# A new stored order for an attention and spatial-gate kernel on one core

## The chip, the cores and the metric

The kernel runs on one core of one Trainium2 chip. Its time is what the device takes for one execution, in microseconds (us); the median of three runs stands for the kernel before.

## The reference

```python
# q, k, v: (8 batches, 8 heads, 576 positions, 64)
# coarse attention: q, k, v averaged over groups of 4 positions
out_d = softmax(scale * q_d @ k_d.T) @ v_d          # 144 positions
out_up = repeat(out_d, 4)
# local attention: only positions with |i - j| < 4
out_local = softmax(where(mask, scale * q @ k.T, -1e9)) @ v
x = (out_up + out_local) as (8, 576, 512)
# gated unit over 576 positions
h = gelu(x @ w_in)                                  # (8, 576, 1024), tanh form
u, v = h[..., :512], h[..., 512:]
v_n = layer_norm(v) * g_ln
v_s = einsum('ts,bsd->btd', w_sg, v_n) + b_sg       # mixes positions
out = x + (u * v_s) @ w_out
```

## The kernel before

**Stages.** The attention goes by pairs of heads, 32 in all, numbered 4 times the batch plus the pair. For one pair the kernel loads four arrays (q, k, two forms of v), sums q and k over groups of four positions (lines 596 to 600), multiplies scores for both attentions into banks of PSUM (lines 625 to 653), adds the mask (640), takes maxima (662 to 676), exponentials (692 to 714), sums and reciprocals (719 to 725), normalises (728, 736), transposes by matmuls (739, 748), copies out of PSUM (248), multiplies with v (800, 816) and adds the two results (781 to 787, 823). The gated unit goes by batches: 931 (924 in the first batch) multiplies into v, 1132 and 1143 into u, 1086 mixes the positions with w_sg, 1267 multiplies with w_out, 1274 adds x. Every float32 product is made of products of a rounded high part and a low part, so many pieces are splits of an array: a cast (248) and a subtraction (835, 1021, 1250, 424, 535).

**Pieces and their names.** A program is 2,448 pieces; a name is a kind, a number and sometimes a chunk. Those that the prediction speaks of: `D1` is the product with v of pair 1, and the products of `D9` those of pair 9 (lines 800 and 816); `YS10` the coarse and local scores of pair 10 (653 and 632); `ma9` and `mb9` the mask addition (640), `qs10` the sums of q (596), `my9` maxima (674, 676), `od7` a scaling (787), `mx9` maxima (664), `xa7` and `xb7` the addition of two results (823). `v1.2` is a chunk of the second batch's product into v (931), `u1.2` of its product into u (1132), `s1.01` the first product of its mixing of positions (1086). `sa0.4` and `sa0.7` take the first batch's mixed values out of PSUM (1185), and `sa7.4` and `sa7.6` the last batch's (1120), `sm0.4` applies such a value to the gate (1194). `wlr1` and `wbr3` are steps in splitting w_out (424; 407 and 409), `sg` guards the small gain vector of 128 by 4 (339 to 341), `gt` guards the gain row of 64 by 512 and takes its reciprocal (339 to 341, 349), `ta1` to `ta4` combine parts of w_sg (516), `tl` and its like split them (535, 556), `oa0.0` adds x into an output of the first batch (1226). `gd7` and `gl7.1` make a factor of the last batch's output products (1238, 1250), `o7.12` and `s7.14` are products of that batch (1267, 1086).

**What sets the order.** The string `ORDER` holds all pieces in one sequence. `place` (lines 69 to 87) walks through it: each word names a piece and, behind a slash, the engine where there is a choice (V is VectorE, A ScalarE, P GpSimd). A piece that needs a buffer takes the one that has been free for longest, out of 8 banks of PSUM ("ps"), 10 buffers "X" or 38 buffers "R", and the last reader in the sequence gives it back. The loop at lines 1452 to 1460 emits the pieces in that sequence with the automatic scheduler off, so each engine runs its pieces in the order of the string, and a piece waits for its inputs and for the last reader of the buffer that it got. Ahead of `S0` and `S3` the loop puts 28 and 20 matmuls of zeros (line 1459). All loads and stores go out on the queue of SyncE (SP), and each waits for the sixth before it (`DEPTH = 6`).

Of the kernel before, what the change touches and what calls it, by code (L numbers as in the profile page):

```python
# [90 lines left out]
lq0 lk0 ks0 qs0 S0 mx0 ia0 ib0 lk1 ea0 Y0 my0 ny0 lq1 S1 qs1/P lk2 mx1 es0 ia1 lq2 S2 ks1/P ib1 ks2/P qs2/P lq3 lk3 ec0  # L91
re0 rc0 Y1 qs3/P my1 mx2 S3 ea1 es1 nq0 ks3/P wy0 wqy0 wby0 ia2 ib2 ny1 np0 wuy0 ec1 wy2 wqy2 U0 re1 wuy2 lk4 wy1 rc1
wty0 np1 ea2 T0 pa0 pb0 mx3 ia3 ib3 Y2 ks4/P my2 wqy1 pc0 ea3 lv0 es2 T1 t0 ny2 lq4 es3 ec2 pe0 Y3 re2 my3 ny3 pa1 rc2
nq1 t1 lw0 U1 ec3 qs4/P wuy1 pb1/V pc1 wby2 D0 wby1 oe0 od0 re3 rc3 YS4 xa0 pe1 ma4 mb4 wz0 wuz0 xb0 lv1 why0 nq2 np2 U2
wqz0 T2 pa2 wty2 lk5 why2 t2 pb2 np3 T3 wty1 pa3 pc2 lw1 D1 pe2/V nq3 mx4 nx4 eb4 wly2 wz3 wqz3 lv2 ks5 wbz0 oe1/V lq5
lw3 my4 ny4 U3 pb3 ec4 vk0.0 t3 vk3.0 lv3 od1 xa1 xb1 pc3 pe3 qs5 wbz3 wuz3 why1/V ea4 vk0.1 YS5 my5 vk1.0 vk1.1 ny5
wtz0 ec5 wy3 wqy3 lw2 vs2 vk2.0 vk2.1 wtz3 D2 ma5 mb5 mx5 re4/V rc4 wby3 nx5 oe2/V od2 vs3 D3 np4 vk3.1 wuy3 wty3 xa2
xb2 wly0 oe3/V wz1 od3 xa3 vk1.2 xb3 eb5 ea5 lv4 whz3/V wlz3 wuz1 lw4 re5 vk2.2 v0.2 v0.1 whz0/V wlz0 rc5 nq5 vs4/V np5
wqz1 nq4/A vg0.2 t4 why3 U4 wly3 T4 pa4 pb4/V vb0.2/A pc4/V pe4 lk6 ks6 lq6 wz2 vk3.2 wbz1 v0.3 wtz1 lk7 vp0.2 wq2 vg0.1
wqz2 vg0.3 vk0.2 v0.0 vg0.0 ks7/P qs6 vb0.0/A wuz2 wbz2 wtz2 vb0.1/A T5 vp0.1 pa5/V D4 YS6 lq8 U5 oe4/V od4 vk4.0 vk4.1  # L100
# [1422 lines left out]
```

## Time and profile before

| | us |
|---|---|
| runs | 555.56, 552.9, 556.1; median 555.56 |
| profiled execution | 553.21, of which the span is 551.4 |
| TensorE, matmuls | 538.7 busy, 98% of the span |
| VectorE | 475.1 busy, 86% |
| ScalarE | 428.7 busy, 78% |
| GpSimd | 366.4 busy, 66% |

The granted clock of TensorE is 1.00 in all stretches. PE is TensorE, PEld its load of weights, DVE VectorE, ACT ScalarE, POOL GpSimd, SP SyncE. The span of 551.4 us is cut below into five stretches by hand: up to 41 us the first loads, the splits of w_in and the first four pairs; to 95 us the first batch's gated unit; to 152 us the end of that and the splits of w_out and w_sg; to 537 us the batches that follow, all alike; and the last output products. An idle time is put down to whatever the engine's next instruction waited for last.

### The profile page before, as it was taken

What the parts mean: (1) busy time and instruction counts of PE and PEld (TensorE: products, weight loads), DVE (VectorE), ACT (ScalarE), POOL (GpSimd) and SP (SyncE); (2) the same over time, 40 slices, a digit from 0 to 9 for tenths busy, and PEclk for the clock granted to TensorE, in tenths of its full rate; (3) what the DMA queues carried; (4) which work ended last, traced back from release to release, by engine and by line L of the source; (5) the groups of instructions that cost most, each with busy time, mean ns of one, the idle gap of its engine ahead of it and who ended that gap; (6) DMA issues with size and microseconds to landing.
All of it is one profiled execution on the core that took longest, in us unless ns stands there. A gap on an engine that the chain in (4) does not pass through costs nothing.

```text
span 551.4 us, 17280 instructions
## 1 busy us (share of the span) xinstructions
PE 538.7 (98%) x6720; PEld 490.6 (89%) x6720; DVE 475.1 (86%) x970; ACT 428.7 (78%) x1457; POOL 366.4 (66%) x435
## 2 busy tenths in 40 slices
...
GB/s 313 265 308 291 81 195 207 167 68 59 129 153 100 21 172 60 178 23 90 142 129 122 76 171 99 57 50 61 140 147 149 1 102 116 65 1 1 23 65 87
DMA packets 31923, 64.62 MB, mean 117 GB/s; under 512 B 3744, under 2 KB 4768, under 8 KB 31840
## 3 DMA queue, kind: packets, MB, share of 16 engines
...
q14 instruction: 30, 0.25, 0.1%
...
## 4 chain that ended last, share of the span: by engine, by line
PE 82%; DVE 10%; issue 3%; POOL 2%; ACT 1%; DMA 1%; SPq 1%; DVEq 0%; POOLq 0%
PE ps L1086 16%; PE ps L931 16%; PE ps L1267 14%; PE ps L1132 14%; PE ps L924 3%; PE ps L800 3%; PE ps L1143 3%; PE ps L816 3%; PE ps L739 3%; PE ps L632 3%; PE ps L748 2%; PE ps L653 2%; PE ps L1459 1%; DMA X<-in_vw_dram 1%; DVE R L1021 1%
## 5 line engine op out<-in xcount | busy, mean ns | idle before, releaser
L1132 PE MATMUL ps<-X,weight_z 128*128 128x288 f32 x448 | 95.6, 297 | 0.0
L692 ACT ACTIVATE X<-X,nb 128x64 f32<-128x64 f32 x280 | 93.5, 338 | 0.6 <-DVE nb L671 0.2
L931 PE MATMUL ps<-weight_y,X 128*128 128x512 f32 x280 | 84.8, 396 | 0.3 <-DVE R L409 0.3
L1132 PEld LDWEIGHTS ps<-X,weight_z 128*128 128x128 f32 x448 | 73.7, 188 | 0.4 <-DVE R L1226 0.2
L1132 PE MATMUL ps<-R,weight_z 128*128 128x288 f32 x224 | 66.1, 295 | 0.0
L931 PEld LDWEIGHTS ps<-weight_y,X 128*128 128x128 f32 x280 | 51.0, 188 | 10.7 <-PE ps L632 0.4
L1086 PE MATMUL ps<-wsg_h,R 128*128 128x288 f32 x266 | 58.5, 300 | 1.5 <-DVE X L640 0.7
L248 ACT CAST R<-R 128x512 fp32r<-128x512 f32 (+2 forms) x81 | 50.3, 642 | 11.9 <-PE ps L1132 2.3
L1274 DVE TENSOR_TENSOR R<-ps,R 128x288 f32<-128x288 f32 x98 | 42.3, 449 | 19.2 <-PE ps L1267 18.8
L692 ACT ACTIVATION_READ_ACCUMULATOR X<-X,nb 128x1 f32 x280 | 53.2, 190 | 0.0
L1021 POOL TENSOR_TENSOR R<-R,R 128x512 fp32r<-128x512 f32 (+1 forms) x24 | 32.0, 1338 | 28.9 <-ACT R L248 15.2
L1267 PE MATMUL ps<-R,weight_r 128*128 128x288 f32 x336 | 50.7, 296 | 0.0
L1267 PEld LDWEIGHTS ps<-R,weight_r 128*128 128x128 f32 x336 | 47.1, 188 | 1.4
L248 ACT COPY R<-ps 128x464 f32<-128x464 f32 (+4 forms) x94 | 33.5, 395 | 17.4 <-PE ps L739 13.5
L1086 PEld LDWEIGHTS ps<-wsg_h,R 128*128 128x128 f32 x266 | 43.7, 188 | 2.8 <-issue 0.9
L931 PE MATMUL ps<-weight_y,R 128*128 128x512 f32 x112 | 44.3, 396 | 0.0
L728 POOL TENSOR_TENSOR X<-X,rc 128x640 f32<-128x640 f32 x25 | 33.1, 1325 | 14.7 <-DVE rc L725 11.6
L1132 PEld LDWEIGHTS ps<-R,weight_z 128*128 128x128 f32 x224 | 42.2, 188 | 0.0
L1166 ACT ACTIVATE R<-ps 128x288 f32<-128x288 f32 x64 | 24.1, 414 | 23.1 <-PE ps L1132 21.4
L1250 POOL TENSOR_TENSOR R<-R,R 128x576 fp32r<-128x576 f32 x19 | 29.0, 1535 | 15.3 <-ACT R L248 9.6
L1267 PE MATMUL ps<-R,R 128*128 128x288 f32 x252 | 37.5, 298 | 0.0
L613 DVE TENSOR_REDUCE vd<-R 112x128 f32<-112x512 f32 x36 | 37.3, 1076 | 0.0
...
## 6 DMA issues: line engine op xcount, KB each, us to landing
...
```

The costliest lines, as they stand in the source:

```text
L248: (nc.scalar.copy if e == "A" else ENG[e].tensor_copy)(**kw)
L613: nc.vector.tensor_reduce(out=vd[:, i], in_=v.rearrange("p f d -> p d f"), axis=AX.X, op=ALU.add)
L692: nc.scalar.activation(out=st["ms"][:, t, :], in_=src, func=AF.Exp, bias=st["nb"][:, t:t + 1], scale=scale, accum_out=sums[par][:, t:t + 1])
L728: ENG[e].tensor_tensor(out=st["ms"], in0=st["ms"], in1=bc_last(st["rc"][:, 0:NT], KB), op=ALU.mult)
L931: nc.tensor.matmul(out=acc, lhsT=r32(l), rhs=r32(weights[f"y{k}"][:, 0, w]), start=(i == 0 and ks[0] == 0), stop=(i == len(ops) - 1 and ks ...
L1021: ENG[e].tensor_tensor(out=r32(dst), in0=vact[s][0][0:n], in1=vh[0:n, 0:DM], op=ALU.subtract)
L1086: nc.tensor.matmul(out=s_bank(j, c), lhsT=r32(l), rhs=r32(r), start=first_in and i == 0, stop=i == len(ops) - 1, skip_group_check=not firs ...
L1132: nc.tensor.matmul(out=acc[:, 0:HALF], lhsT=r32(l), rhs=r32(r), start=(first and n == 0), stop=(last and n == len(ops) - 1))
L1166: nc.scalar.activation(out=gate(i), in_=at["ps", "m", b, "u", i][:, 0:HALF], func=AF.Gelu_apprx_tanh)
L1250: ENG[e].tensor_tensor(out=r32(gl[m]), in0=us[raws[m]], in1=gh[m], op=ALU.subtract)
L1267: nc.tensor.matmul(out=bank(j, c), lhsT=r32(l), rhs=r32(r), start=first and i == 0, stop=i == len(ops) - 1, skip_group_check=not first)
L1274: nc.vector.tensor_tensor(out=x, in0=bank(j, c), in1=x, op=ALU.add)
```

## The change

The string `ORDER` is replaced in whole, lines 91 to 213; no other line differs. The pieces are the same 2,448. Their sequence differs: 558 of them stand more than 20 places from where they stood, 201 at most. 346 of them run on another engine: 101 go from VectorE to ScalarE, 85 from ScalarE to VectorE, 76 from GpSimd to VectorE, 60 from VectorE to GpSimd, 13 from GpSimd to ScalarE and 11 from ScalarE to GpSimd. Since buffers are handed out along the string, other pieces share a buffer. One line of the table before and one now, both from its end:

```diff
--- before.py
+++ after.py
@@ -88,123 +88,123 @@
 
 
 ORDER = """
...
-o7.15 ua7.6 sa7.6 gl7.0 o7.11 sa7.4 gh7.1/A gd7/V gh7.4/A gl7.1/V oa7.15 o7.05 o7.02 gl7.4/V o7.01 os6.2 os6.1 gh7.6/A
...
+ua7.6 gl7.3/V s7.04 s7.14 sa7.6 sa7.4 gh7.1/A gd7/V os6.1 o7.01 gl7.1/V oa7.00 gl7.4/V o7.15 o7.05 oa7.15 gh7.6/A o7.12
...
```

Three places in the order follow. A row is a line of the program, an operation, what it writes and reads (with the number of the buffer and of its use) and the tile's shape.

**VectorE near the end of the first batch's mixing of positions**, before. Lines 674 and 676 are `my9`, 823 `xa7` and `xb7`, 596 `qs10`, 424 `wlr1`, 339 to 341 `sg`, 1185 `sa0.7`, which frees the bank that `YS10` gets, and 407 and 409 `wbr3`, which frees the bank of `v1.2`:

```order
L674 TENSOR_REDUCE stats1_94<-ps2_1702 128x2
L676 TENSOR_REDUCE stats1_94<-ps4_1703 128x1
L823 TENSOR_TENSOR R34_1809<-ps1_1672,od21_92 128x5x58
L823 TENSOR_TENSOR R34_1809<-ps5_1673,od21_92 128x5x58
L596 TENSOR_REDUCE qd0_89<-R11_1806 128x144
L424 TENSOR_TENSOR weight_r1_1773<-R24_1244,weight_r1_1773 128x2x256
L339 TENSOR_SCALAR g_tmp_78<-g_sb_74 128x4
L340 SCALAR_TENSOR_TENSOR g_tmp_78<-g_sb_74,g_tmp_78 128x4
L341 TENSOR_TENSOR g_sb_74<-g_sb_74,g_tmp_78 128x4
L1185 SCALAR_TENSOR_TENSOR wst3l_121<-ps6_1836,g_sb_74,wst3h_75 128x288
L407 TENSOR_SCALAR ps7_1855<-weight_r3_1635 128x512
L409 SCALAR_TENSOR_TENSOR R13_1856<-weight_r3_1635,ps7_1855 128x512
```

and now (the first row is `sa0.4`, the second `mx9`):

```order
L1185 SCALAR_TENSOR_TENSOR wst3l_121<-ps4_1751,g_sb_74,wst3h_75 128x288
L664 TENSOR_REDUCE stats1_94<-X7_1744 128x10
L823 TENSOR_TENSOR R4_1816<-ps6_1673,od21_92 128x5x58
L823 TENSOR_TENSOR R4_1816<-ps7_1674,od21_92 128x5x58
L339 TENSOR_SCALAR g_tmp_78<-g_sb_74 128x4
L340 SCALAR_TENSOR_TENSOR g_tmp_78<-g_sb_74,g_tmp_78 128x4
L341 TENSOR_TENSOR g_sb_74<-g_sb_74,g_tmp_78 128x4
L1194 TENSOR_TENSOR R8_1254<-R8_1254,wst3l_121 128x288
L424 TENSOR_TENSOR weight_r1_1668<-R1_1280,weight_r1_1668 128x2x256
L1185 SCALAR_TENSOR_TENSOR wst3l_121<-ps2_1800,g_sb_74,wst3h_75 128x288
L407 TENSOR_SCALAR ps6_1858<-weight_r3_1615 128x512
L409 SCALAR_TENSOR_TENSOR R16_1859<-weight_r3_1615,ps6_1858 128x512
```

The guard `sg` moved ahead of `wlr1`, and `sm0.4` (line 1194) came to VectorE between them; `qs10` (596), `my9` (674, 676) and `od7` (787), which stood behind `sa0.4`, now stand ahead of it, above the first row shown.

**VectorE between the reciprocal of the gain row and the first batch's output**, before. 516 are `ta1` to `ta4`, 1226 are the additions of x to the first batch's output:

```order
L516 TENSOR_TENSOR R30_2245<-R18_1951 128x288
L516 TENSOR_TENSOR R30_2245<-R26_2243 128x288
L1226 TENSOR_TENSOR R19_618<-ps4_2193,R19_618 128x288
L556 TENSOR_TENSOR wsdl_86<-R27_2085,wsdh_85 64x288
L516 TENSOR_TENSOR R13_2274<-R31_2272,R18_1951 128x288
L516 TENSOR_TENSOR R13_2274<-R5_1949,R26_2243 128x288
L516 TENSOR_TENSOR R11_2277<-R31_2272,R30_2245 128x288
L516 TENSOR_TENSOR R11_2277<-R5_1949,R30_2245 128x288
L516 TENSOR_TENSOR R28_2284<-R31_2272,R11_2277 128x288
L516 TENSOR_TENSOR R28_2284<-R5_1949,R11_2277 128x288
L725 RECIPROCAL rc0_108<-sums0_95 128x13
L535 TENSOR_TENSOR wsg_l_80<-R30_2245,wsg_h_79 128x2x288
```

and now:

```order
L516 TENSOR_TENSOR R26_2234<-R35_2232 128x288
L516 TENSOR_TENSOR R26_2234<-R10_2059 128x288
L516 TENSOR_TENSOR R15_2237<-R28_2000,R26_2234 128x288
L516 TENSOR_TENSOR R15_2237<-R32_2207,R26_2234 128x288
L1226 TENSOR_TENSOR R23_725<-ps7_2194,R23_725 128x288
L516 TENSOR_TENSOR R33_2250<-R28_2000,R35_2232 128x288
L516 TENSOR_TENSOR R33_2250<-R32_2207,R10_2059 128x288
L516 TENSOR_TENSOR R16_2257<-R28_2000,R15_2237 128x288
L516 TENSOR_TENSOR R16_2257<-R32_2207,R15_2237 128x288
L556 TENSOR_TENSOR wsdl_86<-R30_2020,wsdh_85 64x288
L248 CAST wst4h_83<-R16_2257 128x576
L1226 TENSOR_TENSOR R22_713<-ps4_2271,R22_713 128x288
```

The last addition of the first batch, `oa0.0`, reads the bank that `u1.2` gets next; it now stands behind all of `ta1` to `ta4`, line 556 and a cast, and line 535 went elsewhere.

**The queue of loads (SP) for w_sg, the gain row and the bias rows**, before:

```order
L240 DMA R12_1946<-in_b_rows_dram 64x576
L240 DMA R5_1949<-in_w_sgT_dram 128x576
L240 DMA R18_1951<-in_w_sgT_dram 128x576
L240 DMA R20_2002<-in_kT_dram 128x586
L240 DMA R16_2012<-in_qT_dram 128x586
L240 DMA R29_2050<-in_qT_dram 128x586
L240 DMA R27_2085<-in_w_sgT_dram 128x576
L240 DMA R11_2087<-in_v4_dram 112x512
L240 DMA R28_2088<-in_v4_dram 112x512
L240 DMA R33_2135<-in_g_row_dram 64x512
L240 DMA R26_2243<-in_w_sgT_dram 128x576
L240 DMA R31_2272<-in_w_sgT_dram 128x576
```

and now:

```order
L240 DMA R28_2000<-in_w_sgT_dram 128x576
L240 DMA R30_2020<-in_w_sgT_dram 128x576
L240 DMA R32_2039<-in_kT_dram 128x586
L240 DMA R10_2059<-in_w_sgT_dram 128x576
L240 DMA R9_2098<-in_qT_dram 128x586
L240 DMA R37_2135<-in_qT_dram 128x586
L240 DMA R26_2137<-in_v4_dram 112x512
L240 DMA R15_2138<-in_v4_dram 112x512
L240 DMA R17_2166<-in_g_row_dram 64x512
L240 DMA R32_2207<-in_w_sgT_dram 128x576
L240 DMA R35_2232<-in_w_sgT_dram 128x576
L240 DMA R35_2300<-in_b_rows_dram 64x576
```

The bias rows were the first of this stretch and are now the last, in the buffer that a part of w_sg had; the gain row keeps its place behind two loads of v, in a buffer that `D9` reads last.

## Rows read from the trace of the kernel before

**Rows 1.** The page's part 1, all engines: busy us, share of the span, instructions
```profile
PE 538.7 (98%) x6720; PEld 490.6 (89%) x6720; DVE 475.1 (86%) x970; ACT 428.7 (78%) x1457; POOL 366.4 (66%) x435
```

**Rows 2.** Windows, us: busy time (instructions) of each engine, granted clock, DMA share, GB/s
```profile
0.00:41.00 41.00, 35.96 (x722) 26.34 (x723) 33.77 (x95) 30.04 (x114) 32.46 (x50) 1.00 0.92 294
41.00:95.00 54.00, 53.25 (x711) 40.99 (x709) 48.83 (x104) 49.99 (x164) 46.34 (x48) 1.00 0.61 193
95.00:152.00 57.00, 54.16 (x650) 49.85 (x649) 55.42 (x106) 47.33 (x162) 35.43 (x41) 1.00 0.36 110
152.00:537.00 385.00, 384.20 (x4562) 362.51 (x4561) 328.60 (x650) 298.34 (x1016) 247.94 (x295) 1.00 0.29 90
537.00:551.40 14.40, 11.18 (x84) 10.91 (x82) 8.47 (x18) 2.97 (x5) 4.28 (x4) 1.00 0.24 84
```

**Rows 3.** Waits of TensorE, whole span: us in total, times, longest us
```profile
PE ps L653 <- DVE wst3l L1185: 1.6, 1, 1.6
PE ps L739 <- issue: 1.3, 1, 1.3
PE ps L739 <- POOL X L728: 1.2, 2, 0.9
...
PE ps L800 <- issue: 0.8, 1, 0.8
PE ps L1086 <- DVE X L640: 0.7, 1, 0.7
...
PE ps L748 <- POOL pd L736: 0.4, 1, 0.4
```

**Rows 4.** Timeline of TensorE: start, length, work, [idle before <- releaser]
```profile
102.66 0.52 PE L653 MATMUL ps<-kd,qd 64*64 64x144 f32 x12 [1.59 <-DVE wst3l L1185]
...
104.09 0.70 PE L931 MATMUL ps<-weight_y,X 128*128 128x512 f32 x2 [0.26 <-DVE R L409]
...
114.66 0.22 PE L816 MATMUL ps<-R,X 64*64 64x58 f32 x1
...
130.59 1.58 PE L1132 MATMUL ps<-R,weight_r 128*128 128x288 f32 x10 [0.25 <-DVE R L1226]
...
151.44 0.50 PE L1086 MATMUL ps<-wsg_h,R 128*128 128x288 f32 x2 [0.74 <-DVE X L640]
```

**Rows 5.** Timeline of VectorE, around the first wait, columns as above
```profile
95.03 0.52 DVE L1185 SCALAR_TENSOR_TENSOR wst3l<-ps,g_sb,wst3h 128x288 f32<-128x288 f32 x1 [0.62 <-PE ps L1132]
...
99.13 1.39 DVE L339 TENSOR_SCALAR g_tmp<-g_sb 128x4 f32<-128x4 f32 x1
...
102.09 0.52 DVE L1185 SCALAR_TENSOR_TENSOR wst3l<-ps,g_sb,wst3h 128x288 f32<-128x288 f32 x1
```

**Rows 6.** Timeline of GpSimd in the same stretch
```profile
98.77 1.73 POOL L835 TENSOR_TENSOR R<-R,X 128x576 fp32r<-128x576 f32 x1
```

**Rows 7.** Groups of VectorE by line and form: busy us, mean ns
```profile
L596 DVE TENSOR_REDUCE qd<-R 128x144 f32<-128x576 f32 x21 | 15.6, 742 | 0.0
...
L424 DVE TENSOR_TENSOR weight_r<-R,weight_r 128x512 fp32r<-128x512 f32 x2 | 1.4, 684 | 0.0
...
L725 DVE RECIPROCAL rc<-sums 128x13 f32<-128x13 f32 x32 | 7.4, 233 | 2.3 <-ACT sums L719 1.3 <-ACT R L248 0.8
```

**Rows 8.** Timeline of VectorE, the gain row and the second wait
```profile
120.13 0.65 DVE L339 TENSOR_SCALAR R<-R 64x512 f32<-64x512 f32 x1
...
130.10 0.43 DVE L1226 TENSOR_TENSOR R<-ps,R 128x288 f32<-128x288 f32 x1
```

**Rows 9.** Timeline of VectorE in the tail
```profile
537.54 0.76 DVE L1238 TENSOR_TENSOR R<-R,R 128x576 f32<-128x576 f32 x1
538.25 0.76 DVE L1250 TENSOR_TENSOR R<-R,R 128x576 fp32r<-128x576 f32 x1
```

**Rows 10.** DMA view, 90 to 120 us: count, KB each, median us from issue to landing
```profile
R<-in_b_rows_dram SPq DMA_DIRECT2D x1, 144.0 KB, 3.4
R<-in_g_row_dram SPq DMA_DIRECT2D x1, 128.0 KB, 2.7
```

More of the change, by code (lines that the diff above doesn't have):

```diff
@@ L90 @@
 ORDER = """
[L91 to L100, printed above, removed]
@@ L106 @@
-vl0.4/P nx7 eb7 small b xh5/V wlz2 xl5/P D6 YS8 my8 ny8 s0.1 s0.2 ma8 ea7 mb8 oe6/V mx8 nx8 lv7 vs7/V re7 rc7 lq9 od6
-eb8 xa6 sa0.1 ec8 lk10 ks10 s0.0 sa0.0 s0.3 wtr1 sm0.1 np7 T7 pa7 lk9 nq7 ks9 U7 pb7 t7 xb6 sm0.0/P pc7/V lw7 wr3 ea8
-sa0.2 xl4/P pe7 s0.5 re8 wtr2 qs9 wqr3 sa0.3 sm0.3/P rc8 np8 wr0 sm0.2/P wqr0 D7 YS9 nq8/A s0.4 lv8 vs8/V sa0.5 ma9 whr2
-mb9 oe7 lw8 gh0.0/A wur0 gl0.0 sa0.4 whr1 t8 T8 pa8 U8 pb8 xc5 sm0.5/P mx9 od7 xh6 xl6/P pc8 lw9 pe8 my9 lq10 ny9 xa7
-xb7 qs10 wur3 wlr1/V nx9 xh7 ec9 s0.6 s0.7 sg sa0.7 wbr3 D8 YS10 xc6 lv9 xl7/P oe8/V sm0.4/P eb9 vs9 my10 sm0.7 sa0.6 br
@@ L111 @@
-od8 tq3 tq0 v1.0 ma10 wtr3 v1.2 ea9 re9/V rc9 gh0.2/A wbr0 ny10 np9/V ec10 xa8 xb8 lk11 nq9/A vg1.2 t9 lq11 mb10 qs11 T9
-ks11 pa9 U9 pb9 vb1.2/A v1.3 pc9 gh0.1/A xc4 lq12 gl0.2 pe9/V D9 tq4 lv10 ta5/V th5 vg1.0 wlr2/V vg1.3 sm0.6 YS11 mx10
-wtr0 whr0/V gr vp1.2 v1.1 gl0.1/V ma11 gh0.3/A mb11 wlr0 vn1.2/A my11 gl0.3 o0.3 xc7/A o0.2 o0.0 whr3 vb1.0/A vg1.1 nx10
-wlr3 ny11 ec11 mx11 vb1.1/A qs12/P vs10/V ea10 nx11 eb10 re10 gt tq1 ta1/V oa0.0 v1.4 tl5/V o0.1 tq2 ta3/V ta2/V vp1.1
-th1 ta4/V rc10 u1.3 tl1/V vp1.0 oa0.1 th4/V tl4 bd va1.4 oa0.2 u1.5 oe9/V od9 lw11 xa9 xb9 o0.6 vj1.4 lk12 ea11 oa0.3
@@ new lines @@
+vp0.4 vn0.4/A wlq3 lv6 whq1 t6 pe6/V wlq1 u0.0 whz1 vh0.4 wur1 u0.1 ua0.0 vh0.3/V lk8 xh5 lw6 vs6/V D6 lv7 mb7 ua0.7 ks8
+YS8 ua0.1 b vl0.4/P mx7 nx7 xl5 vs7/V vl0.2/P ma8 mb8 mx8 ea7 vl0.3/P small s0.2 s0.0 lk10 wtr1 lq9 eb7 nx8 my8 xc5 re7
+ks10 lk9 wlz1 wlz2 s0.1 rc7 nq7/V np7 ny8 oe6 od6 lq10 ea8 wtr2 sa0.0 s0.3 U7 wr3 ec8 T7 sa0.1 sm0.1/P eb8 qs9 xa6 pa7
+pb7/V sm0.0/P ks9 sa0.3 sm0.3/P xb6 pc7/V xl4/P t7 pe7 sa0.2 s0.5 whr1 sa0.5 lw7 D7 lv8 re8 rc8 wqr3 vs8/V YS9 ma9 qs10
+mb9 xh6 sm0.2/P s0.4 np8 nq8/A my9 gh0.1/A wr0 oe7 od7 wur0 wqr0 gh0.0/A xl6/P ny9 U8 lw9 T8 pa8 sa0.4 s0.7 mx9 xa7 xb7
```

207 lines of the change are left out of this document (111 added, 96 removed).

## The prediction, made before the changed kernel ran

> **What bounds the kernel now.** I read the busy times first, to see how much there is to win at all. TensorE works in 538.7 us of the span's 551.4 [rows 1], and the change leaves every matmul as it is, so at most 12.7 us can be won, and part of that lies before the first matmul and behind the last one. Then the busy times by stretch, to see where the 12.7 are: TensorE idles 5.0 us up to 41 us, 0.75 to 95 us, 2.84 to 152 us, 0.8 in the whole of the next 385 us, and 3.2 in the tail [rows 2]. The long middle is as good as full: whatever is moved there can lose, but hardly win. In the stretch from 95 to 152 us the engine that limits is another: VectorE is busy 55.42 of 57 us [rows 2], so that every piece put ahead of one that TensorE waits for shows in the time. Third, the table of TensorE's waits, to see what ended each: the longest, 1.6 us, is for line 1185 on VectorE; the head has waits of 1.3, 1.2 in two parts, 0.8 (just behind 41 us) and 0.4, in all 3.7 us [rows 3]. Last, the timelines of the two engines around 102 us. TensorE reaches `YS10` at 101.07 and starts it at 102.66; it waits 0.26 more at 104.09, 0.25 at 130.59 and 0.74 at 151.44 [rows 4]. On VectorE the guard `sg`, three operations on 128 by 4 elements, stands in front of `sa0.7`: they fill the time from 99.13 to 102.09 [rows 5], the first of them 1.39 us, and it ends as GpSimd's 1.73 us subtraction ends at 100.50 [rows 6]. A reciprocal of 128 by 13 elements takes 233 ns [rows 7], so the size of the operands does not explain 1.39 us; the other engine does.
>
> **Head, up to 41 us: 0.** TensorE's order hardly changes. On the feeding engines one normalisation of pair 0 goes from GpSimd to ScalarE and the other comes one piece earlier, which ends one wait sooner; against that, the banks of pair 0's transposes and of `D1` are freed behind one or two splits of w_in more on VectorE, which has 13 pieces more and 4 fewer (net 5.2 us by their groups' means) in front of its part for pair 2. VectorE idles 7.2 us in this stretch (41 less 33.77, [rows 2]), part of it before the first load has come; the rest can take up some of the 5.2. The bounds are -3.7 (all waits named above vanish) and +5.2 (no idle moment fits). By my walk along the order `D1` comes 1.5 us sooner and the first products with w_in 0.9 us sooner with 0.8 us of work put off, so even; I take zero.
>
> **From 41 to 95 us: 0.** TensorE is busy 53.25 of 54 us [rows 2], and the one wait in it is counted with the head.
>
> **From 95 to 152 us: -1.4.** Five pieces now stand ahead of `sa0.4` (`ma9`, `qs10`, `mb9`, `my9`, `od7`); two of them stood there already. `sa0.4` waited 0.62 us for TensorE before it began at 95.03 [rows 5]; part of the other pieces' time goes into that wait and into idle moments before it, and by my walk it begins about 0.4 later, at 95.4. Behind it come, from start to start, `sa0.4` itself (0.4), `mx9`, `xa7` and `xb7` (1.45 together), `sg` (2.96 from 99.13 to 102.09, [rows 5]), `sm0.4` (0.55), `wlr1` (0.6; 0.68 in [rows 7] with its overlap) and `sa0.7` (0.45 to 0.52). With such a slow `sg`, `sa0.7` ends at 101.8; with one of three times 0.23 (the small reciprocal's time, [rows 7]), near 99.6. TensorE is there at 101.07, so it waits 0.75 or not at all, where it waited 1.59. `wbr3` then ends at 103.2 and the next product, `v1.2`, starts at 103.3 for 104.09 [rows 4]: 0.8 us won with a slow `sg`. I take the slow one, since GpSimd has work at that place in both orders and the only row of it is slow.
>
> [...]
>
> From `v1.2` on TensorE has 46.35 us of work to `s1.01` (151.44 less 104.09, less the waits 0.25 and 0.74, [rows 4]). In between lies `u1.2`, whose bank `oa0.0` frees. On VectorE `oa0.0` now stands behind all of `ta1` to `ta4`, line 556 and a cast, while line 535 left; from the end of `wbr3` to the end of `oa0.0` I add up 27.06 us by the groups' means, less 2.4% by which neighbours overlap: 129.6, a little sooner than the 130.53 of before [rows 8]. TensorE would be there at about 129.25, so 0.35 us of wait. `s1.01` then starts at 103.3 + 46.35 + 0.35 = 150.0 in place of 151.44, provided that the 0.74 us for the mask addition goes, which now stands early enough by my walk. That is -1.4. Bounds: -2.85 (all four waits of [rows 4] gone) and, from the rival below, +2.1.
>
> **From 152 to 537 us: 0.** There is 0.8 us of idle time to win [rows 2]. Upwards, if the new order lost time there at the rate of the second stretch (0.75 per 54 us), it would be 5.3; nothing in the rows points that way, and I keep it as the bound.
>
> **The tail: +0.4.** `sa7.6` and `sa7.4` (0.5 us each) now wait for the batch's last product, `s7.14`, and `gd7` and `gl7.1` follow on VectorE (0.76 each, less overlap 1.5, [rows 9]): 2.6 us. TensorE has three chunks of 0.79 us to do meanwhile, 2.4 us, and then needs that factor for `o7.12`; 0.2 to 0.4 us of wait. Before, these pieces were ready in time. Bounds: 0 and +2.4.
>
> **Sum:** 0 + 0 - 1.4 + 0 + 0.4 = -1.0, from the profiled execution's 553.21 to 552.2. The median of the three runs, 555.56, stands 2.35 above the profiled one, and the three lie 3.2 apart; I add half of the gap and give **553.4 us** for the median of the changed kernel.
>
> **Rival 1: the head gains too.** The waits in the head (3.7 us, [rows 3]) end with normalisations on GpSimd or with no named releaser, and one of these pieces left GpSimd. If all go, the sum is -4.7: 548.5 for a profiled execution, 549.7 for a median. Against it: VectorE gets more work there.
>
> **Rival 2: a backlog on VectorE, slower.** Ahead of `sa0.4` the order has 18 pieces more (8.74 us by the means of their groups, such as 742 ns for a sum of q, [rows 7]) and 14 fewer (5.27): 3.5 us more work on VectorE in the first 95 us. The forecast lets that go into the 5.2 us that VectorE idles from 41 to 95 us (54 less 48.83, [rows 2]). If the idle moments stand where no piece can use them, `sa0.7` ends 3.5 us later than 101.8, at 105.3, `YS10` waits 4.2 us, and `s1.01` starts at 153.5: +2.1, and with the tail's bound 2.4 the sum is +4.5: 557.7 profiled, 558.9 for a median; by less than that, say +2.1 and +0.4, 555.7 and 556.9. It decides as soon as over 1.4 us of the 3.5 find no idle time. What feeds it in the same stretch are the loads: the gain row now waits for `D9`, whose products run until 114.9 [rows 4], and takes 2.7 us to land [rows 10], so 117.6, where VectorE wants it at 120.13 or up to 2 us sooner [rows 8]; the bias rows (3.4 us, [rows 10]) come after `ta3` has read their buffer. A backlog and a late gain row would not add up, since the first hides the second.
>
> **Rival 3: nothing moves.** What is won at `YS10` is waited for again at `u1.2` and `s1.01`, since VectorE limits the stretch as a whole: 553.2 profiled, 554.4 for a median.
>
> **How the numbers follow.** About 1% (5.6 us) is what a measurement of this kernel can tell from no change. Chances: the forecast 0.45, rival 1 0.15, rival 2 0.25 in all its sizes, rival 3 0.15. The range reaches from rival 1's 549.7, a little lower for the scatter of the runs, to rival 2's 558.9: 549 to 559. Faster by over 1% is below 550.0, which takes rival 1 nearly whole: 0.16. Slower by over 1% is above 561.1, which only rival 2 with losses in the long stretch reaches: 0.11. The rest, 0.73, lies within.
>
> **What would show it.** In the profile after: the wait of line 653 for line 1185 shorter than 0.8 us; `sa0.7` ending near 101.8 on VectorE, with the length of `sg`'s three operations beside what GpSimd does then; a small wait before `u1.2`; `s1.01` near 150.0; the busy share of TensorE over the long stretch still above 99.5%; and a wait of some 0.3 us for line 1250 in the output products of the last batch. I am wrong if VectorE's pieces from 41 to 95 us run late as a whole, if the loads of the gain row or the bias rows end a wait of VectorE, or if the head's waits move by over 1.5 us in either direction.

## The result

The changed kernel takes 548.55 us (median of 4 runs, 548.01 to 548.84) beside 554.37 for the kernel before (4 runs); the ratio is 0.990 with an interval of 0.986 to 0.993. Two later comparisons of the same two kernels, with 12 runs of the changed one each, gave 0.993 (0.990 to 0.996) both times. So the change makes the kernel 0.7 to 1.0% faster. The forecast was 553.4 us, a fall of 0.4%, with a range from 549.0: the sign was right, the size was too small (in the profiled executions the forecast had a fall of 1.0 us, where 5.2 were measured), and the time lies under the range by 0.45 us; the two later medians, 549.34 and 548.99, lie at its lower end. Three of the twelve runs of one kernel below, "new to 37 us, then old", took 559.9 to 563.7 us and are left out of its median and its ratio.

### The profile page after: what moved, and what is told of

The parts are those of the page before. It is cut to its first block, busy times and chain, and to the rows that moved or that the text cites. A ratio compares the mean times of both kernels' runs of the same rounds, so it can differ in the third digit from the quotient of the medians.

```text
span 546.2 us, 17258 instructions
## 1 busy us (share of the span) xinstructions
PE 536.2 (98%) x6720; PEld 489.8 (90%) x6720; DVE 475.3 (87%) x978; ACT 433.2 (79%) x1469; POOL 345.0 (63%) x418
## 4 chain that ended last, share of the span: by engine, by line
PE 84%; DMA 8%; DVE 4%; ACT 2%; issue 1%; SPq 0%; ACTq 0%
PE ps L1132 21%; PE ps L1086 17%; PE ps L931 17%; PE ps L1267 14%; DMA R<-in_kT_dram 3%; PE ps L800 3%; PE ps L739 3%; PE ps L816 2%; DMA R<-in_v_dram 2%; PE ps L632 2%; PE ps L748 2%; PE ps L653 2%; DMA weight_y<-in_w_in_dram 1%; DMA weight_z<-in_w_in_dram 1%; PE ps L1143 1%
## 5 line engine op out<-in xcount | busy, mean ns | idle before, releaser
L248 ACT CAST R<-R 128x576 fp32r<-128x576 f32 (+2 forms) x87 | 54.5, 644 | 11.4 <-DVE R L1238 4.0
L248 ACT COPY R<-ps 128x464 f32<-128x464 f32 (+4 forms) x96 | 35.0, 398 | 18.2 <-PE ps L739 8.4
L1250 POOL TENSOR_TENSOR R<-R,R 128x576 fp32r<-128x576 f32 x23 | 33.5, 1467 | 18.6 <-ACT R L248 9.4
L1021 POOL TENSOR_TENSOR R<-R,R 128x512 fp32r<-128x512 f32 (+1 forms) x20 | 27.5, 1375 | 22.6 <-ACT R L248 10.5
L714 ACT ACTIVATE pd<-ps,nbd 128x144 f32<-128x144 f32 x96 | 35.4, 378 | 1.9 <-DVE nbd L683 1.4
L1267 PEld LDWEIGHTS ps<-R,R 128*128 128x128 f32 x252 | 34.7, 188 | 0.5
```

The lines of the kernel that those rows point to most:

```text
L248: (nc.scalar.copy if e == "A" else ENG[e].tensor_copy)(**kw)
L714: nc.scalar.activation(out=pd[:, n], in_=st["sdv"][n].rearrange("p (c k) -> p c k", c=3), func=AF.Exp, bias=st["nbd"][:, n:n + 1], scale=s ...
L1021: ENG[e].tensor_tensor(out=r32(dst), in0=vact[s][0][0:n], in1=vh[0:n, 0:DM], op=ALU.subtract)
L1250: ENG[e].tensor_tensor(out=r32(gl[m]), in0=us[raws[m]], in1=gh[m], op=ALU.subtract)
L1267: nc.tensor.matmul(out=bank(j, c), lhsT=r32(l), rhs=r32(r), start=first and i == 0, stop=i == len(ops) - 1, skip_group_check=not first)
```

## The profile after

The profiled execution took 548.01 us with a span of 546.2, 5.2 less than before. The page's first part for the changed kernel, as in [rows 1]:

```profile
PE 536.2 (98%) x6720; PEld 489.8 (90%) x6720; DVE 475.3 (87%) x978; ACT 433.2 (79%) x1469; POOL 345.0 (63%) x418
```

and its windows, as in [rows 2], the last one cut at the span's end:

```profile
0.00:41.00 41.00, 37.74 (x770) 27.23 (x770) 38.03 (x102) 31.52 (x121) 32.98 (x50) 1.00 0.90 292
41.00:95.00 54.00, 53.41 (x681) 41.81 (x680) 50.92 (x107) 50.99 (x164) 47.31 (x48) 1.00 0.65 201
95.00:152.00 57.00, 57.00 (x680) 53.66 (x679) 53.83 (x107) 53.76 (x188) 32.88 (x41) 1.00 0.39 119
152.00:537.00 385.00, 382.15 (x4553) 361.39 (x4552) 328.54 (x657) 296.98 (x999) 229.03 (x281) 1.00 0.28 87
537.00:546.20 9.20, 5.94 (x45) 5.71 (x43) 4.03 (x10) 0.00 (x0) 2.78 (x2) 1.00 0.46 160
```

Idle time of TensorE is what is left of each stretch: 3.26 us up to 41 us (5.04 before), 0.59 to 95 us (0.75), none to 152 us (2.84), 2.85 in the long stretch (0.80), 3.26 behind it (3.22). In all 2.7 us less. The other 2.5 us are in the busy time, 538.7 to 536.2. Of these, 1.4 are the zero matmuls ahead of the first scores, which took 6.13 us before and 4.75 now (more on them below). For the other 1.1 us I have no cause: the busy time is 0.7 us less from the start of `v1.2` to that of `s1.01` (46.36 to 45.66) and 1.1 us less behind it, against 0.7 us more ahead of `v1.2`. `s1.01` starts at 145.28, where it started at 151.44.

TensorE's waits, as in [rows 3] (total, times, longest):

```profile
PE ps L1267 <- DVE R L1274: 1.5, 1, 1.5
PE ps L931 <- DVE R L1110: 1.4, 1, 1.4
PE ps L1459 <- DVE mask_sb L311: 1.0, 1, 1.0
PE ps L800 <- DVE R L409: 0.6, 1, 0.6
PE ps L1143 <- ACT pd L714: 0.6, 1, 0.6
PE ps L632 <- DMA R<-in_kT_dram: 0.5, 1, 0.5
PE ps L739 <- POOL X L728: 0.4, 1, 0.4
```

The waits for line 1185 and for the mask addition are gone, and those of the head are fewer. Two new ones head the list, of 1.5 and 1.4 us, at 384 and 166 us. Where [rows 5] had the guard `sg` in 2.96 us, VectorE now shows `sa0.4`, the three operations of `sg`, and `sa0.7`:

```profile
93.62 0.52 DVE L1185 SCALAR_TENSOR_TENSOR wst3l<-ps,g_sb,wst3h 128x288 f32<-128x288 f32 x1
...
95.51 0.17 DVE L339 TENSOR_SCALAR g_tmp<-g_sb 128x4 f32<-128x4 f32 x1
95.72 0.17 DVE L340 SCALAR_TENSOR_TENSOR g_tmp<-g_sb,g_tmp 128x4 f32<-128x4 f32 x1
95.92 0.16 DVE L341 TENSOR_TENSOR g_sb<-g_sb,g_tmp 128x4 f32<-128x4 f32 x1
...
96.97 0.51 DVE L1185 SCALAR_TENSOR_TENSOR wst3l<-ps,g_sb,wst3h 128x288 f32<-128x288 f32 x1
```

GpSimd in the same stretch, where [rows 6] had a subtraction running over the guard's start:

```profile
94.00 1.47 POOL L1209 TENSOR_TENSOR R<-R,R 128x576 fp32r<-128x576 f32 x1
96.49 1.87 POOL L835 TENSOR_TENSOR R<-R,X 128x576 fp32r<-128x576 f32 x1 [1.02 <-ACT X L248]
```

GpSimd is idle from 95.47 to 96.49, and the guard takes 0.17, 0.17 and 0.16 us in that gap. `sa0.7` ends at 97.48; TensorE comes for its bank at 98.45, does not wait, and starts `v1.2` at 99.63:

```profile
98.45 0.29 PE L653 MATMUL ps<-kd,qd 64*64 64x144 f32 x1
...
99.63 0.74 PE L931 MATMUL ps<-weight_y,X 128*128 128x512 f32 x2
```

The first row begins the scores of pair 10 (line 653, no wait before it); the second is `v1.2`, at 104.09 in [rows 4]. From there VectorE stays ahead: the gain row's guard starts at 113.80 for 120.13, and `oa0.0` runs at 123.15 for 130.10 [rows 8]:

```profile
113.80 0.42 DVE L339 TENSOR_SCALAR R<-R 64x512 f32<-64x512 f32 x1
...
123.15 0.44 DVE L1226 TENSOR_TENSOR R<-ps,R 128x288 f32<-128x288 f32 x1
```

## The experiments

All times are medians in us; each ratio is to the kernel before on the same chip, with its 95% interval. "New" and "old" are the changed table and the one before. A mixed table takes the first words of one and then all pieces that are left, in the sequence of the other:

```diff
-ORDER = old
+ORDER = new[:188] + [w for w in old if name(w) not in names(new[:188])]
```

| kernel | median | ratio | interval |
|---|---|---|---|
| new, three comparisons | 548.55, 549.34, 548.99 | 0.990, 0.993, 0.993 | 0.986 to 0.993; 0.990 to 0.996 twice |
| new to 37 us, then old (9 runs) | 552.36 | 0.998 | 0.995 to 1.001 |
| new to 92 us, then old | 554.68 | 1.004 | 1.002 to 1.006 |
| new to 150 us, then old | 550.17 | 0.995 | 0.992 to 0.997 |
| old to 37 us, then new | 549.59, 549.07 | 0.993, 0.995 | 0.990 to 0.995; 0.993 to 0.997 |
| old to 93 us, then new | 551.68, 550.25 | 0.997, 0.996 | 0.994 to 1.000; 0.994 to 0.999 |
| old to 150 us, then new | 554.33 | 1.003 | 1.000 to 1.006 |
| old, guard behind `wbr3` | 552.01 | 0.998 | 0.996 to 1.000 |
| old, guard ahead of `my9` | 553.10 | 1.001 | 0.999 to 1.003 |
| old, 10 zero matmuls ahead of `U0` | 554.29 | 1.001 | 0.999 to 1.003 |
| old, both this and the guard behind `wbr3` | 553.14 | 1.000 | 0.997 to 1.002 |
| old, `nq0` on ScalarE | 552.52 | 0.998 | 0.995 to 1.000 |
| new, `nq0` on GpSimd | 549.83 | 0.995 | 0.992 to 0.997 |
| new, two late waits attacked | 548.50, 547.42 | 0.991, 0.990 | 0.988 to 0.994; 0.987 to 0.994 |

### Which part of the order gives the time

New head (188 words) ahead of the old order. 

> The first 188 words of the new table (to about 37 us), then all other pieces in the old sequence. Theory (the head's gain stands by itself): the head's idle time falls from 5.0 to about 3.3 us and the products of pair 1 and later start 2.5 us or more earlier; the time is 0.994 to 0.997 of before. Rival (VectorE sets the time up to the first batch's end, so the head's gain is waited for again): the wait before the scores of pair 10 grows from 1.6 to 3 us or more and the ratio is 0.999 to 1.001. The zero matmuls in front of the first scores took 6.13 us before and 4.75 after: if that goes with the order of the head it is about 4.8 here, if it is chance it may be either.

Old head ahead of the new order. 

> The first 188 words of the old table, then all other pieces in the new sequence. Theory: what the head gave (1.8 us of idle time, with the zero matmuls 3.2) is lost again, what the stretch from 95 to 152 us gave is kept: 0.993 to 0.996 of before, 2 to 3 us above the changed kernel. Rival (the gain comes from the stretch from 95 us alone): as the changed kernel, 0.990. TensorE's idle time from 95 to 152 us is under 0.5 us by the theory. The zero matmuls: 6.1 us if the head's order sets their time, either value if it is chance.

New order to 152 us. 

> The first 708 words of the new table (to about 150 us), then all other pieces in the old sequence. Theory (all of the gain is made before 152 us, and the two new waits of 1.4 and 1.5 us at 166 and 384 us belong to the new sequence behind it): faster than the changed kernel by about 2 us, 0.986 of before, TensorE's idle time from 152 us to the tail under 1 us. Rival (such waits are made anew by any order, since an operation of VectorE now and then runs 1 to 3 us long beside GpSimd): as the changed kernel, 0.990, with waits of over 1 us in other places.

The new head by itself gave 0.998, which its interval does not tell from nothing; its wait before the scores of pair 10 was 1.62 us, so the rival's longer wait did not come. TensorE came to that place at 98.96, 2.1 us ahead of the 101.07 of before, but lost 1.0 us of it in a new wait at 454 us (the last section shows what VectorE did ahead of it). With the old head the new order kept most of the gain, and no idle time from 95 to 152 us. The new order to 152 us gave 0.995: faster than before, and not faster than the whole new table, so the theory's 0.986 fell. Its two waits did go, and one of 1.0 us at 451 us came instead, with 0.5 us at the seam.

> The changed kernel itself, beside the following ones on one chip. Theory (the changed order leaves fewer places where a long run of VectorE beside GpSimd reaches TensorE): 0.990 of before, and its runs lie within 2 us of one another where those of before lie within 6 or more. Rival (the first measurement was of a lucky set of runs): over 0.994, with as wide a spread as before.

> The first 708 words of the old table (to about 150 us), then all other pieces in the new sequence. Theory A (what the new order gains it gains before 152 us; behind it it has two waits of 1.4 and 1.5 us more and 0.7 less): 1.001 to 1.004 of before. Theory B (the gains of the parts add up, and the new order to 152 us alone gave 0.9946 where the whole gave 0.9899): 0.994 to 0.997. The profile tells by the waits of 1 us and more behind 152 us and by TensorE's busy time.

The changed kernel's runs lay from 548.4 to 553.6 here, those of before from 551.1 to 558.0: narrower, but not within the theory's 2 us. The new order behind 152 us gave 1.003, in the range of theory A and at the limit of its interval. That number carries more than the order, though. The mean granted clock of each run is on record, and all twelve runs of this kernel lie below 0.999 (0.985 to 0.997), as do 22 of the 30 of the kernel before. At one mean clock, 0.991, it took 554.3 us (median of 4 runs) and the kernel before 554.7 (3 runs), so a loss behind 152 us is not shown by the ratio. The traces have a small one: from the start of `s1.01` to the end the kernel before takes 400.0 us, this kernel 400.2, and the changed kernel 400.8 to 401.9 in its three profiles. Since `s1.01` starts 6.2 us sooner in the changed kernel, what is won is won ahead of it.

> The first 445 words of the old table (to about 93 us), then all other pieces in the new sequence. Theory (the stretch from 95 to 152 us is where the gain is made, the guard being short there): TensorE's idle time there under 0.5 us in place of 2.84, 0.992 to 0.995 of before, as with the old head alone (0.9925). Rival (the new order between 41 and 95 us had to put VectorE ahead first): idle time of 1.5 us or more in that stretch and 0.996 or more.

> The old first 188 words and the new order behind, a second time. Theory (the new order gains between 41 and 95 us by starting the batch's last pieces with VectorE ahead): 0.992 to 0.994 again and at least 0.2% below the next kernel. Rival (the difference was one of chips and of the clock in the old head): this and the next within 0.15% of each other, both 0.993 to 0.997.

> The old first 445 words (to 93 us) and the new order behind, a second time. Theory: 0.996 to 0.998. Rival: within 0.15% of the kernel before it.

> The new first 445 words (to about 92 us), then the old order. Theory (41 to 95 us gains by itself): 0.995 or less, under the new head alone (0.9976). Rival (the gain is in the order behind 95 us, where the old order has VectorE late): 0.997 to 0.999 as with the new head alone, with 1.5 us or more of wait before the scores of pair 10.

The old order up to 93 us with the new one behind has no idle time from 95 to 152 us in either measurement, and gives 0.996 to 0.997; the old head alone gives 0.995 on the same chip, within 0.15%, as the rival had it. The new order up to 92 us alone is slower than before, 1.004, which neither side had expected. So the stretch from 95 to 152 us is the one that carries the gain. Its size can be read from the traces: the 1.85 us of wait ahead of `v1.2` are gone, and from the start of `v1.2` to that of `s1.01` TensorE takes 45.6 to 45.7 us in all eleven profiles with the new order there, where it took 47.35 before (47.3 to 49.1 in the nine with the old one). I estimate it at 3.5 us, 0.6%, of which the idle time of 2.84 us in [rows 2] is the larger part.

What the new head adds is not told apart by the ratios: the old head with the new order behind gave 0.993 and 0.995, the changed kernel 0.990 and twice 0.993, and the intervals overlap. Nor by the traces: the second profile of the old head with the new order, in which the clock did not fall, has a span of 546.5 us, those of the changed kernel 546.2, 547.4 and 546.9. Where the two heads do differ is in the clock, of which more below.

### The guard

Guard behind `wbr3`:

```diff
-... qs10 wur3 wlr1/V nx9 xh7 ec9 s0.6 s0.7 sg sa0.7 wbr3 D8 YS10 ...
+... qs10 wur3 wlr1/V nx9 xh7 ec9 s0.6 s0.7 sa0.7 wbr3 sg D8 YS10 ...
```

> The old table with one piece moved: the guard of the 128 by 4 gain vector stands behind wbr3 instead of ahead of sa0.7. Theory (its 2.75 us stood in front of the bank that the scores of pair 10 need): the waits of 1.59 and 0.26 us at 102.7 and 104.1 go, and the time falls by 1.6 to 1.85 us, 0.997 of before. Rival (VectorE limits the whole stretch, so that the 1.85 us are waited for again before u1.2 or s1.01): 0.999 to 1.001, with waits of over 1 us at 130 or 150 us. [...]

Guard ahead of `my9`:

```diff
-... pc8 lw9 pe8 my9 lq10 ny9 ... s0.6 s0.7 sg sa0.7 wbr3 ...
+... pc8 lw9 pe8 sg my9 lq10 ny9 ... s0.6 s0.7 sa0.7 wbr3 ...
```

> The old table with the guard six places earlier, in front of my9 and still ahead of sa0.7, where GpSimd has no operation running for 0.4 us (96.5 to 96.9 in the profile of before). Theory (the guard is long only where an operation of GpSimd runs): its three operations take 0.8 us or less instead of 2.75, the wait before the scores of pair 10 falls from 1.6 to under 0.3 us, 0.997 of before. Rival (three dependent operations on 128 by 4 cost VectorE 2.5 us wherever they stand): the wait stays at 1.4 us or more, 0.9995 to 1.001.

Behind `wbr3` the guard took 0.45, 0.16 and 0.32 us, and the waits at `YS10` and `v1.2` went; but from `v1.2` to `s1.01` TensorE took 49.04 us in place of 47.35, so that 1.7 of the 1.85 us were given back, 1.02 of them in a wait for VectorE at 107.13, and the gain of 0.2% is at the limit of its interval: the rival holds for the larger part. What held VectorE there is a step of 218 ns in the mean of the kernel before, which here ran beside GpSimd's operations from 102.49 to 105.36 without a gap:

```profile
103.25 2.15 DVE L723 TENSOR_SCALAR sums<-sums 128x13 f32<-128x13 f32 x1
```

With ten more zero matmuls in the head besides (1.000, next part) the wait of 1.02 us came again, at 109.34, as the rival had it. The second kernel shows why the guard is long at all. VectorE there (the guard's three operations, and one 10 us later), and GpSimd:

```profile
95.13 0.16 DVE L341 TENSOR_SCALAR g_tmp<-g_sb 128x4 f32<-128x4 f32 x1
95.33 0.16 DVE L342 SCALAR_TENSOR_TENSOR g_tmp<-g_sb,g_tmp 128x4 f32<-128x4 f32 x1
95.52 1.43 DVE L343 TENSOR_TENSOR g_sb<-g_sb,g_tmp 128x4 f32<-128x4 f32 x1
...
105.27 3.63 DVE L730 TENSOR_TENSOR X<-X,rc 128x640 f32<-128x640 f32 x1
```

```profile
95.50 1.43 POOL L837 TENSOR_TENSOR R<-R,X 128x576 fp32r<-128x576 f32 x1 [0.40 <-ACT X L250]
...
105.36 0.24 POOL L250 CAST X<-R 128x64 fp32r<-128x64 f32 x1
105.55 1.44 POOL L1211 TENSOR_TENSOR R<-R,R 128x576 fp32r<-128x576 f32 x1
106.94 1.28 POOL L419 TENSOR_TENSOR R<-R,weight_r 128x512 int32<-128x512 int32 x1
```

Two operations of the guard pass in 0.16 us each while GpSimd is idle. The third starts at 95.52, just behind GpSimd's subtraction at 95.50, and takes 1.43 us, as GpSimd's takes 1.43. The guard's time is that of the neighbour, not its own: the rival is refuted, although the theory's 0.8 us for the three was missed too (1.75), by the third. The wait for line 1185 is gone, with 0.75 us for ScalarE at 100.14 in its place. Yet nothing is won, 1.001: the normalisation at 105.27 (0.82 us at 102.30 in the changed kernel) meets GpSimd's operations, which run from 104.10 to 108.22 without a gap, and takes 3.63 us, and TensorE waits 1.52 us for it at 108.96. Here a change of 2 us in VectorE's phase took one operation out of GpSimd's way (the guard's first, 1.39 us before and 0.16 now) and put another in (3.63 us).

### The head and the clock

Ten zero matmuls ahead of `U0`, in the old table, and the same with the guard moved:

```diff
-WARM = {"S0": 28, "S3": 20}
+WARM = {"S0": 28, "S3": 20, "U0": 10}
```

> The old table with ten matmuls of zeros more, in front of U0, the first transposes of pair 0, so that TensorE works where it waited for np0 at 16 us. Theory (an old head whose zero matmuls ran fast reaches U0 early, waits 1.3 to 1.8 us there, and then runs at the half clock from about 18 to 28 us, as two of the profiles show; the old table's runs mix both kinds): granted clock 1.00 in every stretch of the head, D1 before 29 us, and the upper end of the runs comes down, 0.996 to 0.998 of before. Rival (the spread of the runs comes from waits farther on, and the clock of the head hardly matters to the end): the spread stays as wide, 0.999 to 1.002.

> The old table with the ten zero matmuls in front of U0 and the guard of the gain vector behind wbr3. Theory (the two edits take away two separate losses): 0.994 to 0.996 of before, half of what the changed order gives. Rival (what the guard gave is waited for again at 107 us and before s1.01, as in the run with the guard alone, 0.9982): no better than the bridge alone.

One word of the change undone, and the same word alone:

```diff
-... Y1 rc0 lk3 lq4 nq0/A ib1 my1 S3 ...    (new)
+... Y1 rc0 lk3 lq4 nq0 ib1 my1 S3 ...
-... mx2 S3 ea1 es1 nq0 ks3/P wy0 ...       (old)
+... mx2 S3 ea1 es1 nq0/A ks3/P wy0 ...
```

> The changed kernel with one word undone: nq0, the normalisation of pair 0's coarse scores, on GpSimd again and no longer on ScalarE. Theory (that word is what lets np0 end early enough that TensorE does not wait at U0): np0 ends 0.9 us later, TensorE waits 0.5 to 0.9 us at U0, and the time rises by 0.3 to 1 us, or by 2 or more in executions in which the clock falls behind the wait: 1.001 to 1.004 of the changed kernel's 0.9928. Rival (the earlier loads and the order of np0 do it): no wait of over 0.3 us at U0 and 0.992 to 0.993.

> The old table with one word of the change alone: nq0 on ScalarE in place of GpSimd. Theory: np0 starts up to 0.9 us sooner and TensorE's wait at 16 us shrinks by as much, so that the clock falls in fewer executions: 0.997 to 0.999 of before. Rival (ScalarE's 1.1 us there delays the exponentials of pairs 1 and 2, for which TensorE waits next): 0.999 to 1.002, with longer waits from 19 to 28 us.

The 28 zero matmuls in front of the first scores took between 4.54 and 6.13 us in the profiles, with the old head and with the new alike (4.65 to 6.13, and 4.54 to 5.91): their pace rises, from 6 or 7 in a microsecond to as many as 12, at another moment in each execution, whatever the order (in the changed kernel's profile to 10 from 4 us on; in the profile before it is 6 or 7 up to the last of the 28, and 12 from 13 to 14 us), while the column of the granted clock reads 1.00 throughout; what sets the moment is open. With the old head, an execution in which they are quicker brings TensorE earlier to `U0`, where it waits for the normalisation `np0` on GpSimd. Three profiles have 1.26, 1.38 and 1.81 us of wait there (zero matmuls in 5.30, 4.65 and 4.67 us), and the first and the last then show the half clock (a mean granted clock of 0.991 over the execution in both). TensorE in the kernel "old to 150 us, then new" (zero matmuls in 4.67 us), and windows of it with the granted clock behind the five engines' busy times:

```profile
16.67 0.32 PE L741 MATMUL ps<-turn_l,X 122*128 122x122 f32 x1 [1.81 <-POOL X L730]
...
17.12 0.58 PE L741 MATMUL ps<-turn_l,X 122*128 122x122 f32 x4
...
19.14 1.08 PE L741 MATMUL ps<-turn_l,X 122*128 122x122 f32 x4 [0.18 <-POOL X L730]
```

```profile
16.00:18.00 2.00, 1.33 (x16) 1.17 (x17) 1.55 (x5) 0.90 (x2) 2.00 (x3) 0.92 0.52 135
18.00:20.00 2.00, 1.82 (x20) 1.51 (x13) 1.00 (x3) 2.00 (x6) 1.92 (x3) 0.50 0.73 244
...
26.00:28.00 2.00, 2.00 (x67) 2.00 (x64) 0.31 (x2) 0.50 (x4) 0.52 (x1) 0.52 0.82 255
28.00:30.00 2.00, 2.00 (x60) 1.89 (x56) 1.91 (x6) 1.95 (x5) 1.49 (x2) 1.00 1.01 298
```

After the wait of 1.81 us the granted clock is 0.50 from about 18 to 28 us, and four transposes take 1.08 us where they took 0.58. `D1` then starts at 30.39, where it started at 28.98 in the profile before, with the wait of 0.24 us in that place and no fall (1.00), and at 27.54 in the profile with the wait of 1.38 us, which has no fall either. No profile with the new head shows a fall there: apart from the 1.0 us ahead of its first instruction its longest wait up to 41 us is 0.8 us, and 1.3 with `nq0` back on GpSimd, at 20 us. That one word undone gave 0.9945 against 0.9927 and 0.9928 on other chips, within the theory's range and inside the intervals; the wait at `U0` was 0.24 us, less than the theory's, and the longer one came at the next pair's transposes. Alone in the old table the word left a wait of 1.0 us at `U0` beside quick zero matmuls (4.68 us), where the old word had left 1.38 and 1.81 beside 4.65 and 4.67, and gave 0.998, within the theory's range and not clear of no change.

How often the clock falls is told by the runs. The mean granted clock is 0.991 in the two profiles with the fall in the head, 0.995 and 0.997 in the two with a later fall (next paragraph), and 0.999 or 1.00 in the other sixteen. Of the 230 runs of all kernels with the old head as it was, the kernel before among them, 88 have a mean clock of 0.994 or less; of the 83 with the new head 8; and of the 36 of the three kernels in which the old head had the ten zero matmuls or `nq0` on ScalarE, none. So the old head does cost something, in about four of ten executions, and the bridge and the one word each take that away.

This gives the gain its parts. On the chips of the two later comparisons the changed kernel's median is 4.6 and 3.8 us under that of the kernel before; among the runs with a mean clock of 0.999 or 1.00 it is 2.3 and 3.5 us under it (551.6 to 549.3, 552.1 to 548.6). I take these for what the waits and the work are worth by themselves (the traces' 3.5 us less the 0.9 lost behind `s1.01` are 2.6), and the rest, 2.3 and 0.3 us, for the clock, which falls in fewer executions. The wide spread of the kernel before is in good part the clock's too: at 0.999 or 1.00 its 58 runs lie from 550.8 to 554.2, all 148 from 550.8 to 558.5.

The bridge won nothing even so: expected 0.996 to 0.998, measured 1.001. At a mean clock of 0.999 or 1.00 its runs take 553.5 us (4 runs) beside 552.6 (15 runs), and in its profile the ten matmuls take 1.26 us themselves, and TensorE then waited 1.24 us at 33.7, at the first products with w_in; what ended that wait the trace does not name. Its profile shows a second place at which the clock falls, and the profile of "old, `nq0` on ScalarE" shows the same. There TensorE, and its granted clock:

```profile
101.27 0.52 PE L655 MATMUL ps<-kd,qd 64*64 64x144 f32 x12 [1.60 <-DVE wst3l L1187]
...
102.69 0.90 PE L933 MATMUL ps<-weight_y,X 128*128 128x512 f32 x2 [0.26 <-DVE R L411]
```

```profile
100.00:102.00 2.00, 0.73 (x42) 0.73 (x46) 1.82 (x4) 2.00 (x12) 1.84 (x4) 1.00 0.92 287
102.00:104.00 2.00, 1.74 (x30) 1.40 (x21) 2.00 (x5) 0.84 (x5) 1.70 (x3) 0.76 0.59 204
104.00:106.00 2.00, 2.00 (x7) 1.54 (x6) 1.97 (x7) 0.81 (x5) 1.72 (x2) 0.50 0.50 180
106.00:108.00 2.00, 2.00 (x9) 1.64 (x8) 1.97 (x5) 1.93 (x4) 0.59 (x1) 0.89 0.18 66
108.00:110.00 2.00, 2.00 (x11) 1.55 (x10) 2.00 (x6) 0.39 (x1) 1.25 (x1) 1.00 0.04 8
```

The wait of 1.60 us before the scores of pair 10 is the one of [rows 4]; here the granted clock falls to 0.50 behind it, for 3 to 4 us, and from `v1.2` to `s1.01` it takes 48.66 us where it took 47.35 before, although the 0.25 us before `u1.2` is gone. Of six profiles with that wait two show the fall, [rows 4] among those that do not. So the wait that the forecast priced at 1.59 us costs about 1.5 us more in some executions, which the profile before could not show.

### The two new waits

```diff
-... sa1.6 ks14 xl10 s1.12 sy1.10 zh1 ...
+... sa1.6 ks14 s1.12 sy1.10 xl10 zh1 ...
-... my26 ny26/V o4.17 ... vp5.4 fc5.1/V ua5.1 gl4.6 oa4.12 o4.14 ...
+... my26 ny26 o4.17 ... vp5.4 oa4.12 fc5.1/V ua5.1 gl4.6 o4.14 ...
```

In the changed kernel VectorE, ahead of the wait at 384 us, and GpSimd:

```profile
380.24 3.32 DVE L683 TENSOR_SCALAR nbd<-stats 128x3 f32<-128x3 f32 x1
383.48 0.41 DVE L1041 TENSOR_TENSOR R<-R 128x256 f32<-128x256 f32 x1
383.81 0.44 DVE L1274 TENSOR_TENSOR R<-ps,R 128x288 f32<-128x288 f32 x1
```

```profile
380.06 2.80 POOL L1250 TENSOR_TENSOR R<-R,R 128x576 fp32r<-128x576 f32 x2
382.82 0.72 POOL L1041 TENSOR_TENSOR R<-R 128x256 f32<-128x256 f32 x1
```

An operation on 128 by 3 elements takes 3.32 us, until GpSimd has ended its two subtractions and the one that follows; `oa4.12` (line 1274), which frees the bank, is queued behind it. Ahead of the wait at 166 us it is the same with a subtraction (`xl10`, line 835, 0.74 us at 166.17), behind which `sy1.10` (line 1110) frees the bank:

```profile
162.86 2.96 DVE L835 TENSOR_TENSOR R<-R,X 128x576 fp32r<-128x576 f32 x1
165.75 0.50 DVE L1110 SCALAR_TENSOR_TENSOR R<-ps,g_sb,R 128x288 f32<-128x288 f32 x1
```

```profile
163.03 1.43 POOL L835 TENSOR_TENSOR R<-R,X 128x576 fp32r<-128x576 f32 x1
164.40 0.81 POOL L1123 TENSOR_TENSOR R<-R,R 128x288 f32<-128x288 f32 x1
```

> The changed kernel with its two late waits attacked: xl10 (2.96 us on VectorE beside GpSimd) stands behind sy1.10, whose bank TensorE waited for, ny26 (128 by 3, 3.32 us) goes from VectorE to ScalarE and oa4.12 one place ahead of fc5.1. Theory (each is one operation that GpSimd's run held up, in front of one that frees a bank): both waits go, 2 to 2.8 us less than the changed kernel, 0.985 of before. Rival (the shifted sequence meets GpSimd's runs in other places and waits there): 0.988 to 0.991, with new waits of 1 us or more at other places.

> The changed kernel once more. Theory (most of its gain comes from 95 to 152 us, 0.67%, a smaller part from the head where that is not waited for again): 0.990 to 0.994. Rival (its first measurement was lucky and the parts are all there is): 0.995 to 0.997, as the new order behind an old head gave.

> The version with xl10 behind sy1.10, ny26 on ScalarE and oa4.12 ahead of fc5.1 once more. Theory (the wait of 1.5 us at 384 us is gone for good, that at 166 us was only made smaller, 1.4 to 1.05): 0.1 to 0.3% below the changed kernel, and no run above 552. Rival: within 0.1% of it.

The changed kernel came to 0.993 once more, within its theory. With the two edits the wait at 384 us is gone in both profiles; that at 166 us is 1.0 us instead of 1.4, since the product now waits for `xl10` itself. The version is 0.15 and 0.3% below the changed kernel beside it (548.50 to 549.34, 547.42 to 548.99), with 13 runs from 546.8 to 549.5 where the changed kernel's 24 go up to 553.9. At a mean clock of 0.999 or 1.00, which all 13 have, it is 0.8 and 1.2 us below it. It is the fastest kernel here, though the intervals of the two overlap, and the theory's 0.985 was missed.

## Why the prediction was wrong

The sum had a fall of 1.0 us in the profiled execution, and 5.2 were measured: idle time of -1.8, -0.2, -2.8, +2.05 and 0.0 us in the five stretches, and -2.5 us of busy time.

- **From 95 to 152 us, -1.4: this step failed by its size.** It took the guard at 2.96 us, because the one row of it was slow and GpSimd had work near it in both orders. In the new order the guard meets a gap of GpSimd and takes 0.5 us. The forecast had this as its other value ("near 99.6" for the end of `sa0.7`) and set it aside. VectorE was then 6.3 us early at the gain row, the 0.35 us before `u1.2` did not come, and all of the 2.84 us went; with the busy time that went too, the starts of `v1.2` and `s1.01` put the stretch at 3.5.
- **TensorE's busy time, taken as given: failed.** The sum counted idle time alone, since every matmul stays as it is. The busy time fell by 2.5 us: 1.4 by the zero matmuls, which another execution would have had otherwise, and 1.1 without a cause that I could show. From `v1.2` to `s1.01`, where the sum kept 46.35 us, it is 45.66, and it goes with the order there in every profile in which the clock did not fall.
- **The head, 0: failed.** The walk had `D1` 1.5 us sooner and an even end; it came 4.6 us sooner, at 24.36, and the idle time fell by 1.8 us. This was one of the forecast's own signs of being wrong (waits that move by over 1.5 us). How much of it reaches the end is not shown: the kernels with the old head and the new order behind do not stand clear of the changed one. What is shown was left out of the walk, and no row of that one profile had it: behind waits of 1.26 and 1.81 us the clock fell in two profiles (mean granted clock 0.991) and behind one of 1.38 us it did not, so that the old head's cost differs from run to run.
- **The base: failed.** I added half of the gap between the median and the profiled execution (1.2 us) to the forecast. That gap belonged to three runs: the five later medians of the kernel before are 552.8 to 554.0, the first of them 553.21, the same as its profiled execution. The changed kernel's profiled execution, 548.01, stands 0.5 us from its median.
- **From 41 to 95 us, 0: held.** VectorE's busy time there went from 48.83 to 50.92 us, so its idle moments did take up the added pieces; this is what rival 2 doubted.
- **From 152 to 537 us, 0: failed in the other direction,** with 2.05 us more of idle time, 1.1 us in the run of this part alone (1.91 in place of 0.80). TensorE's busy time behind `s1.01` fell by 1.1 us meanwhile, so that 0.9 us were lost from there to the end. Both waits come from operations of VectorE (2.96 and 3.32 us) that ran beside GpSimd.
- **The tail, +0.4: failed;** no wait of line 1250 appears, idle time there is as before.
- **The loads (under rival 2): no wait** for the gain row or the bias rows.

Rival 1 (head and stretch both gain, 549.7) was the nearest by its number, and had 0.15; that is in part luck, since it had the gain from the waits in the head, and the kernels with the old head kept most of it. What I had wrong as a whole was to add up stretches with one duration for each operation. The trace held the warning in [rows 5, 6], one operation six times as long as its size explains (1.39 us, where the small reciprocal took 0.23), and I used it for one place and not for the others.
